# Queries, keys and values of two head pairs per load in an attention and expert kernel

## The chip, the cores and the metric

The kernel runs on one core of a Trainium2 chip. The time is the device time of one execution in microseconds (us); for the kernel before, the median of three runs is 401.37 us, from 398.73 to 402.49 us. The profile was taken from one more execution, which took 402.86 us. TensorE does the matmuls, VectorE (DVE), ScalarE (ACT) and GpSimd (POOL) the elementwise work, and SP issues most DMAs; GpSimd and ScalarE issue a few. All DMAs of the core share 16 DMA engines.

## The reference

Attention with a relative position bias over 8 batches, 8 heads, 576 positions and 64 values per head in float32; its output goes, token by token, through one of 8 experts that a hash of the token's number picks. Cut to what matters:

```python
scores = q @ k.T / sqrt(64) + bias[:, h]       # bias depends on |i - j| alone
attn = softmax(scores)
x = (attn @ v) as rows of 512 per token        # 4608 tokens
e = token_ids * 2654435761 % 8
out[token] = maximum(x[token] @ w1[e], 0) @ w2[e]
```

## The kernel before, in words

Attention works on pairs of heads: 4 pairs in each of 8 batches, 32 pairs (`pairs`, numbered n = 4b + m). Of a head's 576 positions, 512 form the main part, and the last 64 the rest, which are loaded and treated for all heads of a batch together. The main part of one head lies in memory as 2 blocks (NT = 2) of 128 rows of 512 bytes, each row two positions. A tile `qf`, `kf` or `vf` holds one pair, 256 KB in float32, 2 KB in each of 128 partitions, and each has four buffers. `load(n)` fills it with one DMA per head, 128 KB each, so six DMAs per pair, all but two from SP's queue. `load_rest(b)` loads the rest rows: two DMAs of 64 KB each for `qr` and `kr`, four of 32 KB for `vr`, each tile with a single buffer.

The casts to 16 bits follow. `cast_qk(n)` makes `qh` and `kh` (two buffers each), `cast_v(n)` makes `va` (three), both on GpSimd but for the first pair; `cast_rest` is on DVE and `cast_vrest` on GpSimd. TensorE then transposes `qh` and `kh` (`transpose_qk`), DVE copies the transposes out of PSUM (`kt`, `qt`), and TensorE multiplies them into the scores (`products`). ScalarE takes the exponential of five score tiles per pair (g = 0 to 4, `scores`, line 507), DVE multiplies some of it by bias factors (`band`), and TensorE multiplies the result by the values (`av_steps`, line 575). DVE divides by the sums and writes `x_all`.

The order on every engine is written out by hand (`manual_schedule`); each engine works its own list in order, and waits for what the others owe it. The list is made by a loop over the score tiles. At the first score tile of pair n, `pair_start(n)` issues, in this order: the rest rows of the next batch when m = 0, the loads for pair n + 4, the token numbers' loads at n = 4 (`route_load`, six small DMAs), one of ten fills of a table in device memory (`fill_table`, 514 KB, pairs 2 to 11), the casts of queries and keys for pair n + 3, from n = 12 on two scatters of finished rows by GpSimd (`dispatch`), and near the end the loads of the first two experts' weights by GpSimd's queue: w1 of expert 0 at pair 20, w2 at 22, w1 of expert 1 at 25 and w2 at 28. `behind(n, 2)` casts the values of pair n + 1, and `behind` at pairs with m = 1, g = 3 casts the rest rows of the next batch. `early(n, 3)` transposes the queries and keys of pair n + 2. A load into a buffer that is still to be read waits for the cast that reads it, and what stands behind that load in SP's list waits with it.

Before the loop stands a start by hand: the loads of pairs 0 to 3, the bias table's way through device memory (`btr`, and `btb` in three DMAs), constants and first casts. After the loop, the experts' part loads the scattered rows (`x_load`), and for each expert runs two rows of matmuls (lines 859 and 877), with weights two experts ahead.

Of the kernel before, what the change touches and what calls it, by code (L numbers as in the profile page):

```python
# [11 lines left out]
F32 = mybir.dt.float32  # L12
# [19 lines left out]
def kernel(  # L32
# [11 lines left out]
    nc = tc.nc  # L44

    B, H, S, D = q.shape
# [103 lines left out]
    with tc.tile_pool(name="at", bufs=1) as at, tc.tile_pool(  # L150
# [33 lines left out]
        def load(n, which="qkv", eng=None):  # L184
            b, m = pairs[n]
            for key, dst, src in (("q", qf, q), ("k", kf, k), ("v", vf, v)):
                if key not in which:
                    continue
                dst[n] = at.tile([P, 2, NT, 2 * D], F32, name=key + "f",
                                 bufs=4)  # L190
                for hh in range(2):
                    (eng or nc.sync).dma_start(  # L192
                        out=dst[n][:, hh, :, :],
                        in_=bass.AP(
                            src.tensor, (b * H + 2 * m + hh) * S * D,
                            [[2 * D, P], [2 * P * D, NT], [1, 2 * D]],
                        ),
                    )

        def load_rest(b, which="qkv", eng=None):  # L200
            for key, dst, src in (("q", qr, q), ("k", kr, k)):
# [3 lines left out]
                for hh in range(2):  # L205
                    (eng or nc.sync).dma_start(  # L206
                        out=dst[b][:, hh, :],
                        in_=bass.AP(
                            src.tensor, ((b * H + hh) * S + NB4) * D,
                            [[2 * S * D, NPAIR], [2 * D, RU], [1, 2 * D]],  # L210
                        ),
                    )
# [13 lines left out]
        def cast_qk(n, qeng=None, keng=None):  # L226
            for dst, src, name, eng in ((qh, qf, "qh", qeng),
# [4 lines left out]
                    in_=src[n][:, :, :, :].rearrange(  # L232
# [4 lines left out]
        def cast_v(n):  # L237
            nc.gpsimd.tensor_copy(
                out=va[n % 3][:, :, :D],
                in_=vf[n][:, :, :, :].rearrange(  # L240
# [148 lines left out]
        def transpose_rest(b):  # L389
# [10 lines left out]
            for hh in range(2):  # L400
# [6 lines left out]
                        "p c (m u) -> p c m u", m=NPAIR  # L407
# [7 lines left out]
                    "p c (m u) -> p c m u", m=NPAIR  # L415
# [206 lines left out]
        load(0, "k")  # L622
# [12 lines left out]
        load(0, "q")  # L635
# [26 lines left out]
        load(0, "v", nc.scalar)  # L662
        load_band(0, 2, nc.scalar)
        load(1, "qk")
# [31 lines left out]
        load(1, "v")  # L696
        cast_vrest(0)
        load(2)
        load_band(4, H, nc.sync)
        cast_qk(2)  # L700
        load(3)
        nc.sync.dma_start(out=msk[:, :], in_=MSK_d.ap())
        nc.sync.dma_start(out=cnt[:, :], in_=CNT_d.ap())
        nc.sync.dma_start(out=tok[:, :], in_=TOK_d.ap())

# [25 lines left out]
        def pair_start(n):  # L731
# [3 lines left out]
            if n + 4 < NP:  # L735
                load(n + 4)
# [14 lines left out]
            if n == 20:  # L751
                load_w1(0)
            if n == 22:
                load_w2(0)
            if n == 25:
                load_w1(1)
            if n == 28:
                load_w2(1)
# [270 lines left out]
```

## Time and profile before

| What | Value |
|---|---|
| median of 3 runs | 401.37 us |
| the profiled execution, its own time | 402.86 us |
| its span | 401.1 us |
| TensorE busy in the span | 325.7 us (81%) |
| ScalarE, GpSimd, DVE busy | 205.6, 165.0, 158.5 us |
| exponentials (line 507), 160 of them | 152.6 us busy |
| matmuls of the experts (lines 859 and 877) | 72.4 and 72.7 us busy |
| moved by all DMAs | 72.86 MB in 94548 packets |

Attention takes the span's first 229 us or so, the experts the part from 242 us to 391 us. Busy times are added up over the span, so an engine can be full in one stage and waiting in another; the rows below are read by stretches for that reason.

### The profile page before, as it was taken

How to read it: one execution, taken by the hardware profiler on the slowest of the kernel's cores; microseconds unless marked ns; L12 is line 12 of the kernel's file. 1: busy time of each engine (PE TensorE's matmuls, PEld its weight loads, DVE VectorE, ACT ScalarE, POOL GpSimd, SP SyncE). 2: the span in 40 equal slices, each digit the busy share in tenths (PEclk: the TensorE clock that was granted, in tenths of full speed). 3: DMA queues.
4: the chain of work that ended last, by engine and by line, in shares of the span. 5: the costliest groups of instructions: out<-in, count | busy, mean ns of one | idle time of the engine just before them, and what ended most of it. 6: DMA issues, size and time to landing. Idle time of an engine off the chain costs nothing.

```text
span 401.1 us, 9071 instructions
## 1 busy us (share of the span) xinstructions
PE 325.7 (81%) x3680; PEld 205.3 (51%) x3680; DVE 158.5 (40%) x386; ACT 205.6 (51%) x243; POOL 165.0 (41%) x229
## 2 busy tenths in 40 slices
PE   2664997879798697875978609999999999999990
PEld 0232664456565464643645406565757565656650
DVE  1114464876565656544534401314051322223120
ACT  1472995688968788854957403241505041322310
POOL 6132532424468575592566220233242515141231
PEclk9987998899989999988988957999999999999997
DMA  5896958979794858997959042589999999995221
GB/s 152 203 235 170 283 130 200 256 203 265 210 256 135 253 158 180 270 158 203 211 160 168 16 157 88 94 193 158 270 176 226 229 176 266 162 262 112 91 72 61
DMA packets 94548, 72.86 MB, mean 182 GB/s; under 512 B 15223, under 2 KB 85655, under 8 KB 94496
## 3 DMA queue, kind: packets, MB, share of 16 engines
q1 hardware_dynamic: 74720, 40.13, 37.5%
q0 software_dynamic: 17664, 30.96, 36.6%
q10 hardware_dynamic: 2112, 1.09, 1.0%
q8 instruction: 31, 0.51, 0.5%
q14 instruction: 21, 0.17, 0.1%
HBM read 69.47 MB, written 21.03 MB: 226 GB/s over the span
## 4 chain that ended last, share of the span: by engine, by line
PE 56%; DMA 19%; SPq 12%; DVE 5%; issue 3%; POOL 2%; ACT 1%; ACTq 0%; POOLq 0%; DVEq 0%
PE hps L859 17%; PE ops L877 17%; PE px L575 6%; SPq L192 6%; DMA qf<-in_q_dram 5%; PE ps L465 5%; PE ps L442 4%; DMA kf<-in_k_dram 3%; DMA t_xperm<-zx 3%; PE xps L838 2%; DMA vf<-in_v_dram 2%; SPq L218 2%; PE pqk L377 2%; SPq L206 1%; DMA btb<-t_f 1%
## 5 line engine op out<-in xcount | busy, mean ns | idle before, releaser
L507 ACT ACTIVATE att<-ps 128x1024 f16<-128x1024 f32 x160 | 152.6, 1037 | 57.1 <-PE ps L465 44.0
L865 ACT ACTIVATE h<-hps 128x640 f16<-128x640 f32 x64 | 45.0, 704 | 113.4 <-PE hps L859 113.0
L877 PE MATMUL ops<-w2t,h 128*128 128x512 f16 x320 | 72.7, 379 | 0.0
L859 PE MATMUL hps<-xpt,w1t 128*128 128x320 f16 x512 | 72.4, 302 | 0.1
L575 PEld LDWEIGHTS <-att 128*128 128x128 f16 x1408 | 57.5, 101 | 11.6 <-issue 6.8
L885 POOL DMA_INDIRECT out_dram<-ok,xpn x40 | 39.2, 979 | 57.4 <-DVE ok L884 51.3
L575 PE MATMUL px<-va,att 128*128 128x65 f16 x1280 | 61.0, 199 | 1.0 <-issue 0.4
L859 PEld LDWEIGHTS <-w1t 128*128 128x128 f16 x512 | 50.6, 99 | 21.4 <-issue 0.3
L442 PE MATMUL ps<-btb,idents 128*128 128x384 f16 (+1 forms) x256 | 50.0, 283 | 2.2 <-DMA btb<-t_f 1.5
L465 PE MATMUL ps<-qt,kt 64*128 64x512 f16 x256 | 47.1, 414 | 4.5 <-DVE rnk L320 2.0
L600 POOL DMA_INDIRECT t_xperm<-x_all,ds x40 | 40.4, 1010 | 21.0 <-DVE rcp L584 9.4
L230 POOL CAST qh<-qf 128x512 f16<-128x512 f32 x31 | 20.2, 653 | 67.8 <-DMA qf<-in_q_dram 52.2
L877 PEld LDWEIGHTS <-h 128*128 128x128 f16 x320 | 30.7, 98 | 33.5
L884 DVE COPY ok<-ops 128x512 f32<-128x512 f32 x40 | 27.7, 692 | 47.0 <-PE ops L877 47.0
L842 DVE COPY xpt<-xps 128x640 f16<-128x640 f16 x32 | 15.0, 489 | 74.6 <-PE xps L838 60.0
L517 DVE TENSOR_TENSOR att<-att,ebd 128x768 f16<-128x768 f16 x64 | 38.3, 599 | 6.5 <-ACT ebd L540 6.5
L383 DVE COPY kt<-pqk 128x512 f16<-128x512 f16 x32 | 13.6, 425 | 55.9 <-PE pqk L377 46.0
L585 DVE TENSOR_TENSOR x_all<-px,rcp 128x384 f16<-128x384 f32 x64 | 31.4, 491 | 2.2
L442 PEld LDWEIGHTS <-idents 128*128 128x128 f16 x336 | 21.5, 102 | 19.1 <-issue 16.0
L465 PEld LDWEIGHTS <-kt 64*128 64x128 f16 x512 | 16.2, 96 | 29.4 <-issue 22.9
L133 POOL DMA_DIRECT2D w1t<-in_moe_w_dram x8 | 6.5, 807 | 52.3 <-PE xps L838 52.3
L230 POOL CAST kh<-kf 128x512 f16<-128x512 f32 x31 | 19.5, 629 | 13.6 <-DMA kf<-in_k_dram 13.3
(77 smaller groups left out, 264.4 us busy)
## 6 DMA issues: line engine op xcount, KB each, us to landing
kf<-in_k_dram SPq DMA_DIRECT2D x64, 128.0 KB
qf<-in_q_dram SPq DMA_DIRECT2D x64, 128.0 KB
w1t<-in_moe_w_dram POOLq DMA_DIRECT2D x8, 1024.0 KB
w2t<-in_moe_w_dram POOLq DMA_DIRECT2D x8, 1024.0 KB
vf<-in_v_dram SPq DMA_DIRECT2D x62, 128.0 KB
t_xperm<-zx SPq DMA_DIRECT2D x10, 514.0 KB
xpn<-t_xperm SPq DMA_DIRECT2D x8, 642.5 KB
vr<-in_v_dram SPq DMA_DIRECT2D x32, 32.0 KB
```

What stands on the lines that cost most here:

```text
L230: (eng or nc.gpsimd).tensor_copy(out=dst[n][:, :, :, :].transpose([0, 2, 1, 3]), in_=src[n][:, :, :, :].rearrange("p h t (c d) -> p h (t c ...
L442: nc.tensor.matmul(out=out, lhsT=idents[:, which, :], rhs=rhs, start=start, stop=True, skip_group_check=True,)
L465: nc.tensor.matmul(out=ps[:, hh, o : o + rhs.shape[1]], lhsT=lhsT, rhs=rhs, start=not biased and (g < KT or t == 0), stop=True, skip_group ...
L507: nc.scalar.activation(out=att[:, g, :, :], in_=ps[:, :, :], func=AF.Exp, bias=0.0, scale=scale,)
L517: nc.vector.tensor_tensor(out=a, in0=a, in1=ebd[:, 2 * m : 2 * m + 2, 1 - c : 3 - c, :], op=ALU.mult,)
L575: nc.tensor.matmul(out=po, lhsT=lhsT, rhs=rhs, start=(i == 0), stop=(i == len(todo) - 1), skip_group_check=True,)
L585: nc.vector.tensor_tensor(out=x_all[:, b, its[0] : its[0] + ni, :DM].rearrange("p t (m h d) -> p t m h d", h=2, m=NPAIR)[:, :, m, :, :], i ...
L600: sc_in = nc.gpsimd.indirect_dma_start(out=xperm_d.ap()[:, :], out_offset=bass.IndirectOffsetOnAxis(ap=ds2[:, B * t + b : B * t + b + 1], ...
L859: nc.tensor.matmul(out=hps[:, nr, :NR], lhsT=w1h[:, kt, ts(ft, P)], rhs=xt[e][:, kt, ts(nr, NR)], start=(kt == 0), stop=(kt == NPT - 1),)
L865: nc.scalar.activation(out=h1[:, ft, :].rearrange("p (r n) -> p r n", r=NRC), in_=hps[:, :, :NR], func=AF.Relu, bias=0.0, scale=1.0,)
L877: nc.tensor.matmul(out=ops[:, :], lhsT=h1[:, ft, ts(kc, P)], rhs=w2h[:, ft, :], start=(ft == 0), stop=(ft == NFT - 1),)
L885: so = nc.gpsimd.indirect_dma_start(out=out[:, :], out_offset=bass.IndirectOffsetOnAxis(ap=xn[e][:, kc, DM:XW].bitcast(I32), axis=0), in_= ...
```

## The change

A tile `qf`, `kf` or `vf` now holds two pairs (four heads), 4 KB in each partition, with three buffers. A load fills it with one DMA for each of the two blocks T, with four heads in it, 256 KB each; the first two pairs are still loaded as two halves of two heads. In the loop, the loads stand at every second pair: those of queries and keys for pairs n + 6 and n + 7, those of values for n + 4 and n + 5. The casts read their half of the tile. In `load_rest`, the source's order becomes row first, pair of heads second, and the copies behind the rest rows' transposes follow it. The experts' first weights are loaded at pairs 22, 24, 26 and 28 (w1 and w2 of expert 0, w1 and w2 of expert 1). The arithmetic is the same.

```diff
-        def load(n, which="qkv", eng=None):
-            b, m = pairs[n]
+        def load(j, which="qkv", eng=None, h0=0, h1=4):
...
-                dst[n] = at.tile([P, 2, NT, 2 * D], F32, name=key + "f",
-                                 bufs=4)
-                for hh in range(2):
+                if j not in dst:
+                    dst[j] = at.tile([P, 4, NT, 2 * D], F32, name=key + "f",
+                                     bufs=3)
+                for T in range(NT):
                     (eng or nc.sync).dma_start(
-                        out=dst[n][:, hh, :, :],
+                        out=dst[j][:, h0:h1, T, :],
                         in_=bass.AP(
-                            src.tensor, (b * H + 2 * m + hh) * S * D,
-                            [[2 * D, P], [2 * P * D, NT], [1, 2 * D]],
+                            src.tensor, (4 * j + h0) * S * D + 2 * P * D * T,
+                            [[2 * D, P], [S * D, h1 - h0], [1, 2 * D]],
                         ),
                     )
@@ load_rest
-                            [[2 * S * D, NPAIR], [2 * D, RU], [1, 2 * D]],
+                            [[2 * D, RU], [2 * S * D, NPAIR], [1, 2 * D]],
@@ cast_qk (and cast_v with vf)
-                    in_=src[n][:, :, :, :].rearrange(
+                    in_=src[n // 2][:, 2 * (n % 2) : 2 * (n % 2) + 2].rearrange(
@@ transpose_rest, twice
-                        "p c (m u) -> p c m u", m=NPAIR
+                        "p c (u m) -> p c m u", m=NPAIR
@@ the start
-        load(0, "k")
+        load(0, "k", None, 0, 2)
...
-        load(0, "q")
+        load(0, "q", None, 0, 2)
...
-        load(0, "v", nc.scalar)
+        load(0, "v", nc.scalar, 0, 2)
         load_band(0, 2, nc.scalar)
-        load(1, "qk")
+        load(0, "qk", None, 2)
...
         load_rest(0, "v")
-        load(1, "v")
+        load(0, "v", None, 2)
         cast_vrest(0)
-        load(2)
+        load(1, "qk")
         load_band(4, H, nc.sync)
         cast_qk(2)
-        load(3)
+        load(1, "v")
         nc.sync.dma_start(out=msk[:, :], in_=MSK_d.ap())
         nc.sync.dma_start(out=cnt[:, :], in_=CNT_d.ap())
         nc.sync.dma_start(out=tok[:, :], in_=TOK_d.ap())
+        load(2, "qk")
@@ pair_start
             if b + 1 < B and m == 0:
                 load_rest(b + 1)
-            if n + 4 < NP:
-                load(n + 4)
+            if n % 2 == 0 and n + 6 < NP:
+                load(n // 2 + 3, "qk")
+            if n % 2 == 0 and n + 4 < NP:
+                load(n // 2 + 2, "v")
...
-            if n == 20:
-                load_w1(0)
-            if n == 22:
-                load_w2(0)
-            if n == 25:
-                load_w1(1)
-            if n == 28:
-                load_w2(1)
+            if n >= 22 and n % 2 == 0 and n < 30:
+                (load_w2 if n % 4 == 0 else load_w1)((n - 22) // 4)
```

## Rows read from the trace of the kernel before

**Rows 1.** Stretches: length, busy us of engines (x instructions), TensorE's clock, DMA share, GB/s.

```profile
core 0: us, PE busy (x) PEld busy (x) DVE busy (x) ACT busy (x) POOL busy (x), PEclk, DMA share, GB/s
0.00:40.00 40.00, 20.50 (x166) 9.86 (x167) 10.11 (x29) 16.91 (x21) 12.63 (x33) 0.88 0.74 190
40.00:230.00 190.00, 154.81 (x2523) 103.75 (x2521) 105.72 (x285) 143.68 (x159) 99.75 (x141) 0.93 0.79 196
40.00:110.00 70.00, 59.78 (x982) 39.98 (x980) 42.70 (x118) 58.41 (x67) 26.89 (x45) 0.94 0.86 221
110.00:150.00 40.00, 33.84 (x558) 22.81 (x559) 23.93 (x63) 30.98 (x36) 28.94 (x40) 0.96 0.70 201
...
70.00:80.00 10.00, 7.95 (x104) 4.73 (x103) 8.37 (x24) 6.82 (x9) 4.30 (x8) 0.83 1.07 257
90.00:100.00 10.00, 9.72 (x177) 6.73 (x173) 6.87 (x18) 8.76 (x11) 4.85 (x8) 1.00 1.14 266
120.00:130.00 10.00, 8.91 (x157) 6.01 (x153) 5.84 (x14) 8.29 (x11) 8.72 (x12) 1.00 0.46 137
...
245.00:391.00 146.00, 145.90 (x966) 88.51 (x965) 40.08 (x67) 45.05 (x64) 47.81 (x51) 1.00 0.79 171
```

**Rows 2.** Waits, whole span: engine, line, what was waited for, us, times, longest.

```profile
POOL qh L230 <- DMA qf<-in_q_dram: 52.2, 17, 7.6
...
POOL kh L230 <- DMA kf<-in_k_dram: 13.3, 17, 3.9
```

**Rows 3.** TensorE in order of time: start, length, instructions, idle before.

```profile
23.00 0.40 PE L377 MATMUL pqk<-idents,kh 128*128 128x128 f16 x4 [2.10 <-POOL kh L230]
```

**Rows 4.** GpSimd in order of time, same columns.

```profile
111.46 0.61 POOL L230 CAST kh<-kf 128x512 f16<-128x512 f32 x1 [0.65 <-DMA kf<-in_k_dram]
...
153.58 0.84 POOL L133 DMA_DIRECT2D w1t<-in_moe_w_dram  x1
```

**Rows 5.** Instructions on the query tile: count, shortest, median, longest in ns.

```profile
L192 SPq DMA_DIRECT2D qf<-in_q_dram x64: 367/468/2227, 1.7 to 200.9; - x64
```

**Rows 6.** Waits of SP's queue: the first whole span, the second 13 to 30 us.

```profile
SPq L192 <- POOL va L238: 10.3, 4, 3.7
...
SPq L703 <- DMA btb<-t_f: 0.9, 1, 0.9
```

**Rows 7.** SP's queue in order of time: start, length, issues.

```profile
21.34 0.47 SPq L654 DMA_DIRECT2D btb<-t_f  x1
...
27.32 0.34 SPq L703 DMA_DIRECT2D cnt<-t_cnt  x1
```

**Rows 8.** The chain that ended last, in order of time: start, us, what.

```profile
30.27 4.72 DMA kr<-in_k_dram
...
62.25 4.76 DMA t_xperm<-zx
67.03 5.34 DMA qf<-in_q_dram
...
154.26 9.02 DMA vf<-in_v_dram
...
193.74 9.70 DMA kf<-in_k_dram
```

**Rows 9.** SP's DMA queue on the page: packets, MB, share of 16 engines' span.

```profile
q1 hardware_dynamic: 74720, 40.13, 37.5%
```

**Rows 10.** Groups by shape, copies behind the rest rows' transposes: busy us, mean ns.

```profile
L401 DVE COPY kzr<-pr 64x256 f16<-64x256 f16 x16 | 4.6, 289 | 1.5 <-PE pr L393 1.3
...
L410 DVE COPY qtr<-pr 128x256 f16<-128x256 f16 x8 | 2.3, 292 | 0.1
```

**Rows 11.** DVE in order of time, the rest rows' cast.

```profile
35.11 0.29 DVE L250 CAST krh<-kr 128x256 f16<-128x256 f32 x1 [2.25 <-DMA kr<-in_k_dram]
```

**Rows 12.** The chain on the page, shares of the span by engine.

```profile
PE 56%; DMA 19%; SPq 12%; DVE 5%; issue 3%; POOL 2%; ACT 1%; ACTq 0%; POOLq 0%; DVEq 0%
```

More of the change, by code (lines that the diff above doesn't have):

```diff
@@ L239, in cast_v @@
                 out=va[n % 3][:, :, :D],
-                in_=vf[n][:, :, :, :].rearrange(
+                in_=vf[n // 2][:, 2 * (n % 2) : 2 * (n % 2) + 2].rearrange(
                     "p h t (c d) -> p (h t c) d", c=2
@@ L414, in transpose_rest @@
                 in_=pr[:, 1, :, :].rearrange(
-                    "p c (m u) -> p c m u", m=NPAIR
+                    "p c (u m) -> p c m u", m=NPAIR
                 ),
```

## The prediction

> **What bounds the kernel now.** I read the stretches of the span first, then the chain of waits, then the queues. In the stretches [rows 1] the reader is to see two halves. From 245 us on, the experts keep TensorE busy for 145.90 of 146 us; no row says that loads of queries, keys or values reach there, and I leave it as it is. From 40 to 230 us, attention, TensorE is busy for only 154.81 of 190 us (0.81), while the DMA engines stand at 0.79. Neither is full on average. But both are nearly full at times: TensorE 0.97 in 90 to 100 us, and the DMA engines 1.07 and 1.14 in 70 to 80 and 90 to 100. A stage in which two resources take turns at being full is short of work in flight, not of rate.
>
> The waits say who is short: GpSimd stands 52.2 us in 17 waits before its cast of the queries, and 13.3 us before that of the keys, each time for a DMA [rows 2]. The casts feed TensorE's transposes. At 23.00 us TensorE had been idle for 2.10 us until the cast keys of pair 2 came [rows 3]. Even where the DMA engines have room (110 to 150 us, share 0.70), the cast at 111.46 us waited for keys again [rows 1, 4].
>
> Why are the loads late? Two reasons, both on SP's queue. First, an issue takes a median of 468 ns on SP [rows 5], and a pair needs six of them, 2.8 us, besides 8 smaller ones per batch and a table fill. Second, an issue waits for the landing of the eighth one before it: the load of `cnt` at 27.32 us waited 0.9 us for the `btb` of 21.34 us, and from that one to it there are six L192 issues, `msk` and `cnt` itself, eight steps [rows 6, 7]. The chain repeats this: the fill issued at 62.25 us lands 4.76 us later and lets the query load of 67.03 us go, which takes 5.34 us to land, and so on [rows 8]. So eight issues of mostly 128 KB, some 1 MB, share one landing of about 5 us, and any small DMA in the eight costs a whole place. Where the weights come in, at 153.58 us [rows 4], landings grow to 9.02 and 9.70 us [rows 8], and then the lead of the query loads, about two pairs, isn't enough.
>
> **The change, part by part.**
>
> *Larger loads.* Three issues per pair instead of six: 3 x 0.468 = 1.4 us of SP time per pair less. For the issue of 256 KB no row exists; the nearest are 128 KB (468 ns) and the 768 KB `btb` of 21.34 us, 0.47 us [rows 5, 7]. They agree, so I take 0.47. The transfer itself: the rows stay 512 bytes long, so the same number of packets. A price change per packet has no row; the queue's 74720 packets take 37.5% of 16 engines' 401.1 us, 32 ns each [rows 9]. I take no change, and bound it at 10% either way: q, k and v are 55296 packets, 111 us of all 16 engines, so 11 us of DMA time, most of it under other work. What grows is the bytes that eight outstanding issues hold, up to 2 MB.
>
> *Deeper buffers for queries and keys.* Three buffers of two pairs each instead of four of one; a load for pairs n+6 and n+7 now stands at pair n, where the one for n+4 stood. SP runs ahead to whichever buffer is not free: now SP spends 10.3 us waiting for the value casts [rows 6], since value buffer n is freed only in pair n-1. After the change the values for n+4, n+5 need the cast of n-1, which lies in pair n-2, and the queries and keys have five pairs of lead when SP is not behind. At some 5.3 us a pair that is over 25 us, against landings of up to 9.70 us. So GpSimd's waits go nearly entirely. Late next is TensorE's own order, with ScalarE's exponentials beside it (143.68 us of the 190 [rows 1]).
>
> *Rest rows.* The order in the source becomes rows first, heads second. The DVE copies behind the transposes read with a stride then; 16 + 8 copies of 0.29 us [rows 10]: between nothing and twice that, 7 us in all on an engine that is 0.56 busy, taken at 0. For the load: the 64 KB of `kr` took 4.72 us to land, against 5.34 us for 128 KB of queries [rows 8], and DVE stood 2.25 us for it in order, with TensorE behind [rows 11]. I take 1.5 us saved at the start, from 0 to 3.
>
> [...]
>
> *Start.* Pair 2's keys now come with pair 3's, 512 KB more ahead of the cast. At the start's 190 GB/s [rows 1] that is up to 2.8 us, taken 2, on the path at 23.00 us; pair 3 then finds its data there, and I count 1 back. The rest rows of batch 1 have 1 MB more ahead of them on SP's queue: up to 5.5 us at the same rate, though two L192 issues fewer; I take 3, less the 1.5 above. Sum of the start: +2.5, from -1 to +7.
>
> *Weights.* Expert 0's loads move two pairs later, w1 of expert 1 one. GpSimd pays the same issue, 0.84 us for that of 153.58 [rows 4]. By pair 22, SP should have issued nearly all query loads, so the landings of 9 us meet full buffers. They're needed by 245 us, with 50 us to spare, and I cost them at 0.
>
> *The stage.* With the feed in place, what does TensorE reach? [...] (154.8 - 3) / 0.90 = 168.7 us instead of 190: -21.3. The DMA engines must then carry 0.79 x 190 = 150 us in 169, a share of 0.89, below the 1.07 and 1.14 seen.
>
> Sum: -21.3 + 2.5 = -18.8. The profiled execution took 402.86 us for a span of 401.1, so 384.1; it stands 1.5 above the median of 401.37, so **383** beside that median.
>
> **Rivals.**
>
> *The DMA engines remain the bound where they're busy.* From 40 to 110 us their share is 0.86 [rows 1] with the table fills in it, and fuller queues then only lengthen each landing. Against it: 1.07 and 1.14 in two stretches. Then only 110 to 230 us gains: TensorE's 95.0 us there at 0.90 take 105.6 instead of 120, -14.4, and with +2.5 about 389.5 beside the median; 388 to 396 with a smaller gain in it.
>
> *Fully fed.* If 0.95 is held, 160 us, -30 and +2.5: 374; 369 to 378.
>
> *Nothing moves.* The issues that go away were hidden, and the waits only change their name. Against it: SP's queue holds 12% of the chain and the DMAs 19% [rows 12]. Then 397 to 405. [...]
>
> *Slower: dearer packets.* Each issue walks four heads 147 KB apart instead of two blocks 64 KB apart of one head. If a packet of these loads took 40% more than 32 ns, 111 us would become 155, and the stage's 150 us of DMA work 190 or so, all the time there is; with the start's +2.5 and some misses beyond, 408. It decides only above some 35%; below that it eats into the gain. For it: nothing in the rows. Against it: the packets keep length and count.
>
> **Chances.** Within 1% (397.4 to 405.4) is about what a measurement can't tell from no change. My forecast, 378 to 388: 0.42. DMA-bound, 388 to 397: 0.23. Fully fed: 0.13. Nothing moves: 0.13. Slower: 0.09. So faster 0.78. The range of 8 in 10 reaches from 371, most of the fully fed case, to 400, a part of no change. Within the gaining cases the start's bounds (-1 to +7) and 10% on packets move the time by no more than that.
>
> **What would show it.** Right: L192 has 100 issues on SP instead of 190, still near 0.47 us each; GpSimd's waits before L230 fall from 65.5 us to under 15; TensorE's share in attention is near 0.90, DMA's near 0.89; attention ends near 211 us instead of 230; the experts' 146 us unchanged. Wrong: GpSimd waits as long as now at longer landings (DMA-bound); the start's transposes or DVE's rest casts wait over 7 us more; packets above 32 ns; or TensorE's share stays near 0.81 with GpSimd's waits gone, the stage then being bound by its own order.

## The result, and the profile after

The changed kernel took a median of 396.0 us in 17 runs (392.68 to 399.67), the kernel before 402.04 us in 17 beside it: a ratio of 0.9862, 95% interval [0.9829, 0.9895]. That is 1.4% or some 5.5 us, where 383 was forecast and 371 to 400 given as the range. The same file, run again later on two chips, gave 0.9546 [0.9503, 0.9588] and 0.9622 [0.9579, 0.9665], 18.1 and 15.5 us, where 18.8 was forecast. So two questions are open: what kept the gain small in the first comparison, and whether the forecast was right where its number came out. Ratios are those of undisturbed runs alone; one experiment (e3_depth) had one such run and has no ratio.

The profiled execution of the changed kernel took 398.55 us for a span of 396.8. Its stretches, in the columns of [rows 1]:

```profile
40.00:230.00 190.00, 154.51 (x2516) 102.12 (x2513) 115.33 (x285) 142.78 (x158) 100.64 (x139) 0.92 0.76 192
40.00:110.00 70.00, 58.61 (x958) 39.26 (x956) 44.94 (x113) 55.21 (x63) 27.05 (x44) 0.93 0.91 242
...
240.00:386.00 146.00, 145.90 (x966) 88.47 (x964) 40.08 (x67) 45.05 (x64) 47.99 (x51) 1.00 0.79 171
```

Against [rows 1], the reader is to see that TensorE's share from 40 to 230 us did not move (154.51 of 190 after, 154.81 before). The experts' full stretch starts 5 us earlier and is the same 145.90 us. GpSimd's waits, over the whole span, columns as in [rows 2]:

```profile
POOL qh L230 <- PE pqk L377: 39.8, 23, 5.0
...
POOL kh L230 <- DMA kf<-in_k_dram: 4.0, 3, 1.8
POOL qh L230 <- DMA qf<-in_q_dram: 3.9, 2, 2.5
```

The 65.5 us for DMAs [rows 2] have become 7.9. GpSimd now waits for TensorE, 39.8 us of it until a cast tile is given back: the feed is ahead of its user. On the page, SP's DMA queue (packets, MB, share of 16 engines' span) and the chain of waits, to be read against [rows 9] and [rows 12]:

```profile
q1 hardware_dynamic: 73616, 40.13, 37.6%
...
PE 67%; DMA 11%; DVE 7%; SPq 5%; issue 4%; ACT 2%; POOL 1%; POOLq 0%; DVEq 0%; ACTq 0%
```

A packet takes 0.376 x 16 x 396.8 us / 73616 = 32 ns, as before. TensorE's part of the chain rose from 56 to 67%, SP's queue and the DMAs fell from 31 to 16%. What is still late in the changed kernel stands in its order of time, DVE and TensorE (start, length, instruction, idle before):

```profile
9.72 0.39 PE L393 MATMUL pr<-idents,krh 128*128 128x128 f16 x2 [2.42 <-DVE krh L250]
...
35.99 0.40 PE L393 MATMUL pr<-idents,krh 128*128 128x128 f16 x2 [4.36 <-DVE x_all L585]
...
64.89 0.18 DVE L287 TENSOR_SCALAR te<-te 128x40 int32<-128x40 int32 x1 [2.67 <-DMA te<-in_moe_token_ids_dram]
...
66.01 0.38 PE L377 MATMUL pqk<-idents,kh 128*128 128x128 f16 x4 [3.24 <-DVE x_all L585]
```

The rest rows of batch 1 are transposed at 35.99 us after 4.36 us of idle TensorE, and at 64.89 us DVE stands 2.67 us for the small token-number loads, with TensorE idle 3.24 us behind it. Both are small loads that now stand behind larger ones in SP's queue. They were late before as well, though. The rest rows, in the trace of the kernel before:

```profile
36.63 0.39 PE L393 MATMUL pr<-idents,krh 128*128 128x128 f16 x2 [5.06 <-DVE x_all L585]
```

DVE waited 1.53 us for the token numbers there, and 2.40 us in a later trace of the same kernel (f6_before).

### The profile page after: what moved, and what is told of

The parts are those of the page before. It is cut to its first block, busy times and chain, and to the rows that moved or that the text cites. A ratio compares the mean times of both kernels' runs of the same rounds, so it can differ in the third digit from the quotient of the medians.

```text
span 396.8 us, 8968 instructions
## 1 busy us (share of the span) xinstructions
PE 326.2 (82%) x3680; PEld 204.6 (52%) x3680; DVE 169.7 (43%) x386; ACT 205.3 (52%) x243; POOL 165.5 (42%) x229
## 3 DMA queue, kind: packets, MB, share of 16 engines
q1 hardware_dynamic: 73616, 40.13, 37.6%
## 4 chain that ended last, share of the span: by engine, by line
PE 67%; DMA 11%; DVE 7%; SPq 5%; issue 4%; ACT 2%; POOL 1%; POOLq 0%; DVEq 0%; ACTq 0%
PE hps L856 18%; PE ops L874 17%; PE px L575 10%; PE ps L465 8%; PE ps L442 6%; PE pqk L377 4%; PE xps L835 3%; SPq L192 3%; ACT att L507 2%; DMA t_xperm<-zx 2%; DMA qr<-in_q_dram 2%; DVE x_all L585 2%; DMA vf<-in_v_dram 2%; PE ps L499 2%; DMA btb<-t_f 1%
## 5 line engine op out<-in xcount | busy, mean ns | idle before, releaser
L575 PEld LDWEIGHTS <-att 128*128 128x128 f16 x1408 | 56.8, 101 | 11.0 <-issue 5.9
L575 PE MATMUL px<-va,att 128*128 128x65 f16 x1280 | 60.7, 198 | 1.2 <-DVE qt L386 0.5
L856 PEld LDWEIGHTS <-w1t 128*128 128x128 f16 x512 | 50.5, 99 | 21.4 <-issue 0.3
L442 PE MATMUL ps<-btb,idents 128*128 128x384 f16 (+1 forms) x256 | 49.5, 280 | 3.9 <-DMA btb<-t_f 2.9
L600 POOL DMA_INDIRECT t_xperm<-x_all,ds x40 | 41.7, 1042 | 21.1 <-DVE rcp L584 11.1
L465 PE MATMUL ps<-qt,kt 64*128 64x512 f16 x256 | 47.6, 423 | 3.3 <-ACT att L507 3.3
L517 DVE TENSOR_TENSOR att<-att,ebd 128x768 f16<-128x768 f16 x64 | 42.5, 664 | 7.9 <-ACT ebd L540 7.9
L230 POOL CAST qh<-qf 128x512 f16<-128x512 f32 x31 | 19.0, 614 | 46.4 <-PE pqk L377 39.8
L238 POOL CAST va<-vf 128x512 f16<-128x512 f32 x32 | 19.7, 617 | 33.8 <-PE px L575 23.0
L383 DVE COPY kt<-pqk 128x512 f16<-128x512 f16 x32 | 13.6, 425 | 43.8 <-PE pqk L377 41.6
L442 PEld LDWEIGHTS <-idents 128*128 128x128 f16 x336 | 21.0, 101 | 21.7 <-issue 17.2
L465 PEld LDWEIGHTS <-kt 64*128 64x128 f16 x512 | 16.0, 96 | 27.5 <-issue 20.8
L133 POOL DMA_DIRECT2D w1t<-in_moe_w_dram x8 | 6.5, 812 | 51.8 <-PE xps L835 51.8
```

Of the source, the lines that this page charges most:

```text
L442: nc.tensor.matmul(out=out, lhsT=idents[:, which, :], rhs=rhs, start=start, stop=True, skip_group_check=True,)
L465: nc.tensor.matmul(out=ps[:, hh, o : o + rhs.shape[1]], lhsT=lhsT, rhs=rhs, start=not biased and (g < KT or t == 0), stop=True, skip_group ...
L517: nc.vector.tensor_tensor(out=a, in0=a, in1=ebd[:, 2 * m : 2 * m + 2, 1 - c : 3 - c, :], op=ALU.mult,)
L575: nc.tensor.matmul(out=po, lhsT=lhsT, rhs=rhs, start=(i == 0), stop=(i == len(todo) - 1), skip_group_check=True,)
L600: sc_in = nc.gpsimd.indirect_dma_start(out=xperm_d.ap()[:, :], out_offset=bass.IndirectOffsetOnAxis(ap=ds2[:, B * t + b : B * t + b + 1], ...
L856: nc.tensor.matmul(out=hps[:, nr, :NR], lhsT=w1h[:, kt, ts(ft, P)], rhs=xt[e][:, kt, ts(nr, NR)], start=(kt == 0), stop=(kt == NPT - 1),)
```

## The experiments

Theory at the start: the third buffer lets SP run ahead, and the small loads behind it come late (the rest rows, the token numbers), while the cast tiles, still two of each, hold GpSimd. Rival: the DMA engines are the bound. A third theory came from the traces themselves: TensorE's results reach the other engines late. Each series ran on one chip, with the kernel before beside it.

### First series: loads, weights, depth and size alone

**e1_noload** takes the load work away after the first six pairs; the casts then read those pairs' tiles again, so its output is of other data.

```diff
-            if n % 2 == 0 and n + 6 < NP:
-                load(n // 2 + 3, "qk")
-            if n % 2 == 0 and n + 4 < NP:
-                load(n // 2 + 2, "v")
+            if n == 0:
+                load(2, "v")
...
-                    in_=src[n // 2][...
+                    in_=src[n // 2 % 3][...
```

> The changed kernel without the loads of queries, keys and values for pairs 6 to 31; the casts read the first six pairs' tiles again. 23 MB of loads are gone, all else is issued as before. Theory A (attention is bound by the engines' own order, about 6 us a pair, once the loads are ahead): the time falls by 2 to 8 us from the changed kernel's 396, to 388 to 394, mostly from 40 to 100 us, and TensorE's share from 100 to 200 us stays near 0.85. Theory B (the loads are still the bound, by the DMA engines' rate): attention runs at TensorE's 0.95, 20 us or more less, to 376 or under.

Measured: 387.5 us, 0.9621 [0.9544, 0.9698]. With hardly any queries, keys and values left to load, this chip gives 3.8%. One stretch of its trace:

```profile
100.00:170.00 70.00, 60.15 (x1030) 40.10 (x1022) 47.44 (x113) 58.13 (x65) 51.47 (x68) 0.98 0.30 75
```

The DMA engines are at 0.30 there, and TensorE still reaches only 60.15 of 70 us, 0.86. So a lack of transfer rate is not what holds it.

**e2_weights** is the kernel before with only the weights' loads moved.

```diff
-            if n == 20:
-                load_w1(0)
...
-            if n == 28:
-                load_w2(1)
+            if n >= 22 and n % 2 == 0 and n < 30:
+                (load_w2 if n % 4 == 0 else load_w1)((n - 22) // 4)
```

> The kernel before with only the first two experts' weights moved to pairs 22, 24, 26 and 28. Theory A1 (the gain lies from 170 to 220 us because the weights no longer meet the last loads): 2 to 5 us faster than before, ratio 0.988 to 0.995. Rival A2 (the deeper buffers took up the collision, the weights' place is worth nothing): within 1 us of before, ratio 0.997 to 1.003.

Measured: 397.98 us, 0.992 [0.9875, 0.9965]. The move, costed at 0, is worth 0.8% by itself.

**e3_depth** is the kernel before, with its loads of 128 KB, six buffers, and the changed kernel's lead: depth alone.

```diff
-                                 bufs=4)
+                                 bufs=6)
...
-            if n + 4 < NP:
-                load(n + 4)
+            for i in (6, 7) if n % 2 == 0 else ():
+                if n + i < NP:
+                    load(n + i, "qk")
+            for i in (4, 5) if n % 2 == 0 else ():
+                if n + i < NP:
+                    load(n + i, "v")
...
+        load(4, "qk")
+        load(5, "qk")
```

> The kernel before, still with one pair per tile and 128 KB per DMA, but with six buffers and the loads issued where the changed kernel issues them (queries and keys for pairs n+6, n+7 and values for n+4, n+5, at even n). Depth alone. If the places in SP's queue bind (eight issues share a landing), depth can't be filled and the gain is under 2 us, ratio 0.995 to 1.0. If depth is what gave the 6 us, ratio 0.985 to 0.99 with 128 KB DMAs too.

Measured: no ratio, so what depth alone does stays open.

**e4_size** is the changed kernel with two buffers instead of three for queries and keys, so with 256 KB loads and the lead of before. The weights' new places and the rest rows' new order are in it too.

```diff
-                                     bufs=3)
+                                     bufs=3 if key == "v" else 2)
...
-        load(2, "qk")
...
-            if n % 2 == 0 and n + 6 < NP:
-                load(n // 2 + 3, "qk")
+            if n % 2 == 0 and n + 4 < NP:
+                load(n // 2 + 2, "qk")
```

> The changed kernel with two buffers of two pairs for queries and keys (four pairs, as many as the kernel before had) and their loads issued for n+4, n+5 beside the values'. Size alone, without depth. If size gave the gain: 396 or so, ratio 0.983 to 0.99. If depth gave it: GpSimd waits for queries again, over 15 us, and the ratio is 0.993 to 1.005.

Measured: 388.28 us, 0.9683 [0.961, 0.9756], faster than either case had expected. Its GpSimd waits, and TensorE at its first two rest transposes and behind them:

```profile
POOL qh L230 <- DMA qf<-in_q_dram: 31.8, 7, 9.7
POOL kh L230 <- DMA kf<-in_k_dram: 15.2, 11, 2.4
```

```profile
9.65 0.39 PE L393 MATMUL pr<-idents,krh 128*128 128x128 f16 x2 [2.00 <-DVE krh L250]
...
32.44 0.29 PE L393 MATMUL pr<-idents,krh 128*128 128x128 f16 x2 [1.26 <-DVE x_all L585]
...
38.27 0.61 PE L377 MATMUL pqk<-idents,kh 128*128 128x128 f16 x4 [3.53 <-POOL kh L230]
```

GpSimd still waits 47.0 us for loads, against 65.5 [rows 2] and 7.9, and yet the kernel is within 0.6% of the one without loads (which keeps the 1 MB for pairs 4 and 5 at the start). So most of those waits can't have been on the path. The second rest transposes come at 32.44 us instead of 35.99, since the 1 MB no longer stands ahead of the rest rows. But TensorE then idles 3.53 us for the next keys, and the third rest transposes come at 60.41 us, where the changed kernel has 60.48: the 3.5 us are gone again.

### Second series: the late small loads, the cast tiles, the start

```diff
-            if n == 4:
+            if n == 2:
                 route_load()
```

**e5_te** is that edit, the token-number loads two pairs earlier. 

> The changed kernel with the token numbers' loads at pair 2 instead of pair 4. In the changed kernel's trace they land at 64.8 us, DVE waits 2.67 us for them in order, and TensorE stands 3.24 us before the transposes at 66.01 us. Theory A (the deeper prefetch put small urgent loads behind it in SP's queue, and DVE's wait is on the path): 2.5 to 5 us faster than the changed kernel, 391 to 394, ratio to before 0.972 to 0.980. Rival B (the wait is taken up by slack within the next pairs): within 1.5 us of the changed kernel, ratio 0.982 to 0.99.

Measured: 392.89 us, 0.9747 [0.969, 0.9803]; DVE's wait of 2.67 us is gone.

```diff
-                dst[n] = at.tile([P, KT, 2, D], F16, name=name, bufs=2)
+                dst[n] = at.tile([P, KT, 2, D], F16, name=name, bufs=4)
```

**e6_castbufs** is that edit, four cast tiles for two. 

> The changed kernel with four buffers instead of two for the cast queries and keys, so that GpSimd's casts no longer start exactly when TensorE's transposes end, which is when DVE copies these transposes and goes on to line 517 and, at a batch's edge, to the rest rows' casts. Theory A (the casts now run beside DVE's work and slow it: line 517 664 ns against 599, the rest casts 636 against 371): line 517 falls below 630 ns, TensorE's idle time before the rest transposes from 1.91 us each to 1.5 or less, the time by 2 to 5 us, ratio 0.972 to 0.982. Rival B (the collision is off the path): DVE's times fall, the total stays within 1.5 us, ratio 0.982 to 0.99. Rival C: the casts only collide elsewhere, no change in either.

Measured: 393.15 us, 0.9759 [0.9706, 0.9811].

```diff
-        load(2, "qk")
...
                 load_rest(b + 1)
+            if n == 0:
+                load(2, "qk")
```

**e8_start** is that edit, the rest rows of batch 1 ahead of the 1 MB. 

> The changed kernel with the start's loads of queries and keys for pairs 4 and 5 issued behind batch 1's rest rows instead of ahead of them. Theory A (the 1 MB ahead of the rest rows costs the start 3 to 4 us): the first rest transposes come at about 32.5 us instead of 36.0 and the time falls by 2 to 4 us, ratio 0.975 to 0.982. Rival B (the token numbers' landing near 65 us takes it up again): the transposes come earlier, but DVE waits longer for the token numbers and the time falls by less than 1.5 us, ratio 0.982 to 0.99.

Measured: 397.36 us, 0.9881 [0.9832, 0.9931]. The rest transposes came at 32.89 us, as in e4_size, but TensorE then idled 2.73 us for the next keys, at 37.91 us, and DVE waited 2.3 us for the token numbers. It is the slowest of its series: on this chip e5_te is worth more than the earlier rest rows.

**e9_size_rest** is e4_size with the order of the rest rows of before.

```diff
-                            [[2 * D, RU], [2 * S * D, NPAIR], [1, 2 * D]],
+                            [[2 * S * D, NPAIR], [2 * D, RU], [1, 2 * D]],
...
-                    "p c (u m) -> p c m u", m=NPAIR
+                    "p c (m u) -> p c m u", m=NPAIR
```

> The kernel with large loads and two buffers for queries and keys (388.3 us, ratio 0.968) with the rest rows' old order: four heads outermost in the source, and the contiguous copies behind their transposes. [...]

Measured: 391.67 us, 0.9706 [0.9646, 0.9766]. Its first rest transposes:

```profile
13.10 0.40 PE L393 MATMUL pr<-idents,krh 128*128 128x128 f16 x2 [5.33 <-DVE krh L250]
```

They come 3.5 us after those of e4_size (9.65), so the new order does bring the first rest rows sooner. At the fourth rest transposes 0.5 us of it is left (84.59 and 84.09 us). Over the whole kernel 0.9706 and 0.9683, on two chips, can't be told apart.

Read against 0.9862, e5_te and e6_castbufs look like 1% each. But 0.9862 was measured on another occasion, and the next series showed that this is not a fair comparison.

### Third series: repairs together

**e10_te_cast** is e5_te and e6_castbufs together; **e11_size_te_cast** adds the two buffers of e4_size; **e12_oldweights** is the changed kernel with the weights' loads back at pairs 20, 22, 25 and 28; **e13_start_te** is e8_start and e5_te together. Their edits are those above (the weights' in reverse).

> The changed kernel with both repairs: the token numbers' loads at pair 2, and four buffers for the cast queries and keys. Alone they gave ratios of 0.975 and 0.976 against the changed kernel's 0.986, so about 4.5 and 4 us. Theory A (two separate costs, both on the path): they add up, 0.961 to 0.969, 386 to 390 us. Rival B (each only uncovers the other, or the same slack): 0.970 to 0.977.

> The kernel with large loads and two buffers for queries and keys (0.968) with both repairs. In it the token numbers already came in time, and the casts collided less. Theory A: at most 2 us better, 0.962 to 0.970, since only the collision of line 517 (675 ns) is left to take away. Rival B (deeper buffers are needed once the collisions are gone): no better than 0.970.

> The changed kernel with the experts' first weights back at pairs 20, 22, 25 and 28. The weights' new places alone gave the kernel before 0.992. Theory A (with five pairs of lead the loads no longer mind the weights' traffic): within 1.5 us of the changed kernel, 0.982 to 0.990. Rival B (the weights' new places are what gave more than half of the gain in this kernel too): 0.990 to 0.998.

> The changed kernel with batch 1's rest rows ahead of the loads for pairs 4 and 5 at the start (alone 0.988, no gain), and the token numbers' loads at pair 2 (alone 0.975). Theory A (the start's gain of 3 us was taken up by the wait for the token numbers): now it shows, 0.965 to 0.971. Rival B (the start's gain is lost in the wait for the next keys, 2.73 us at 37.91 us in that kernel's trace): no better than the token numbers alone, 0.972 to 0.979.

Measured: e10_te_cast 379.74 us, 0.9571 [0.953, 0.9612]; e11_size_te_cast 377.25 us, 0.9499 [0.945, 0.9548]; e12_oldweights 382.38 us, 0.9647 [0.9598, 0.9696]; e13_start_te 380.5 us, 0.9595 [0.9552, 0.9638]. All four lie below what was expected of them from the ratio of 0.986. What fits least is e12_oldweights: it has none of the repairs and a part of the change less, and was 3.5% faster than before, where the changed kernel had given 1.4%. Either the old place of the weights is better here, against e2_weights, or this chip is another case. So the changed kernel itself had to run again.

### Fourth series: the changed kernel again, and each repair beside it

**f1_after** is the changed kernel without an edit; **f3_size** is e4_size, **f4_te** is e5_te, **f5_castbufs** is e6_castbufs, each again.

> The changed kernel itself, beside its variants on one chip. The series so far ran on three chips, each against the kernel before on the same chip, and the changed kernel itself was in none of them. If the ratio is the same on every chip: 0.983 to 0.990. If it depends on the chip (one series gave its variants 0.957 to 0.965): anywhere from 0.96 to 0.99, and only differences within a series count.

> The kernel with large loads and two buffers for queries and keys, on the same chip as the changed kernel. If the deeper prefetch costs what it seemed to (0.968 against 0.986): 4 to 9 us faster than the changed kernel here. If that was the chip: within 2 us.

> The changed kernel with the token numbers' loads at pair 2, on the same chip as the changed kernel. Theory A: 2.5 to 5 us faster than the changed kernel here. Rival: the 4.5 us found against the changed kernel's ratio were a difference of chips; within 1.5 us here.

> The changed kernel with four buffers for the cast queries and keys, on the same chip as the changed kernel. Theory A (the casts beside DVE's work cost time on the path): 2 to 5 us faster than the changed kernel here. Rival: within 1.5 us, DVE's times fall off the path.

Measured: f1_after 381.38 us, 0.9546 [0.9503, 0.9588]; f3_size 376.93 us, 0.9444 [0.94, 0.9489]; f4_te 382.06 us, 0.9554 [0.9507, 0.96]; f5_castbufs 380.95 us, 0.9534 [0.9492, 0.9576]. Three things follow. The changed kernel gains about what was forecast on this chip. The token numbers' place and the cast tiles are worth nothing that these runs can show. The third buffer is a loss: two buffers are 1.2% faster (376.93 against 381.38), and the intervals don't meet; e11_size_te_cast against e10_te_cast points the same way. The second rest transposes in f1_after, and then in f3_size with what TensorE waits for next:

```profile
36.96 0.28 PE L393 MATMUL pr<-idents,krh 128*128 128x128 f16 x2 [3.43 <-DVE x_all L585]
```

```profile
33.47 0.28 PE L393 MATMUL pr<-idents,krh 128*128 128x128 f16 x2 [1.26 <-DVE x_all L585]
...
38.23 0.40 PE L377 MATMUL pqk<-idents,kh 128*128 128x128 f16 x4 [2.47 <-POOL kh L230]
```

The lead of f3_size is 3.5 us here, but 1.9 us at the third rest transposes (59.74 against 61.65 us), since the wait for keys takes a part of it back, and 4.8 us at the fourth (84.17 against 88.97). From 60 to 90 us f1_after has a granted clock of 0.88 and waits 1.9 us for the token numbers; f3_size has 0.94 and no such wait. So the 1 MB ahead of the rest rows doesn't explain the loss by itself, and e8_start, which takes away just that, was the slowest of its series. Where the third buffer costs its 4.5 us stays open.

### Fifth series: both kernels' traces on one chip

**f6_before** and **f7_after** are the two kernels without an edit.

> The kernel before, unchanged, for its trace on the same chip as the changed kernel's. Ratio to itself 1.00, within 0.5%. Theory of the late completion (VectorE sees the last product of a pair late on some chips): before waits no more than 6.4 us in 30 to 225 us for TensorE ahead of its reciprocal, as in the trace that the prediction rests on, whatever the chip, since its pairs have idle places between them. Rival (the waits belong to the schedule, not to the chip): 6.4 us again within 1 us.

> The changed kernel, unchanged. Theory of the late completion: where the ratio is near 0.986, the trace shows 10 us or more of waits of VectorE's reciprocal for TensorE in 30 to 225 us (10.8 + 3.5 us in the trace on record), and a batch of four pairs takes about 24 us between two rest transposes; where the ratio is near 0.955, it shows none, and a batch takes about 21.5 us. Rival (the difference is one of the kernel before, which is slower on some chips): the ratio differs while the changed kernel's waits and batches are the same. A ratio between 0.965 and 0.977 speaks against two kinds of chip.

Measured: f6_before 397.82 us, 1.0004 [0.9968, 1.004]; f7_after 382.11 us, 0.9622 [0.9579, 0.9665]. In the two traces the last exponentials of the attention end at 218.1 and 204.7 us: 13.4 of the 13.6 us by which the spans differ (393.2 and 379.6) lie in the attention. VectorE's waits ahead of its reciprocal from 30 to 225 us, first in the changed kernel's trace of the first comparison, then in f6_before and f7_after:

```profile
DVE rcp L584 <- PE px L575: 14.2, 22, 3.4
DVE rcp L584 <- PE ps L465: 10.8, 9, 2.4
DVE rcp L584 <- PE ps L442: 3.5, 3, 1.4
```

```profile
DVE rcp L584 <- PE px L575: 13.8, 25, 1.2
```

```profile
DVE rcp L584 <- PE px L575: 11.7, 23, 1.6
```

The reciprocal needs only the products of L575. A wait that ends with a later matmul (L465, L442) means that DVE was let go after TensorE had, by its rows, gone on to other work. There were 14.3 us of those in the first comparison, and none here in either kernel. ScalarE shows it too: its exponentials need scores, which no matmul of L575 writes, and yet some of its waits in that first trace, from 30 to 210 us, end with one. There are none such in f7_after:

```profile
ACT att L507 <- PE px L575: 4.8, 7, 1.8
```

A batch of four pairs, taken between the third and the eighth rest transposes, lasts 24.8 us in the first trace of the changed kernel and 22.2 in f7_after, and 25.4 and 24.9 us in the two traces of before. So the rival of f7_after, that the changed kernel's waits and batches are the same everywhere, falls. The rival of f6_before, 6.4 us of such waits again, falls too: the kernel before has 3.5 + 2.9 us of them in its first trace and none in f6_before. Late results go with the occasion, not with the schedule.

## Why the prediction was right and wrong

**Larger loads: right.** 100 issues on L192 instead of 190, packets at 32 ns. The issue itself has a median of 0.51 us for queries and keys, a little over the 0.47 taken, and of 0.69 for values, half as much again:

```profile
L192 SPq DMA_DIRECT2D qf<-in_q_dram x34: 367/506/1672, 1.7 to 165.6; - x34
L192 SPq DMA_DIRECT2D vf<-in_v_dram x32: 367/688/3887, 15.9 to 176.6; - x32
```

**GpSimd's waits gone: right as a fact,** 65.5 us to 7.9, under the 15 forecast. As a reason it was too much. With 47.0 us of them left, e4_size kept the gain, and f3_size, with 34.5, beat the changed kernel. What counts are the waits that TensorE stood behind, and in the kernel before those were few. From 30 to 225 us, its waits for GpSimd's cast keys and, for comparison, for DVE ahead of the rest transposes:

```profile
PE pr L393 <- DVE x_all L585: 19.2, 7, 5.1
...
PE pqk L377 <- POOL kh L230: 7.4, 4, 2.8
```

Of the 7.4 us, 6.1 stand at 167 us and later, where the weights come in. In the changed kernel TensorE waits for cast keys once, at 23.92 us. The waits ahead of the rest transposes stay: 15.8 us of them in its first trace, 16.6 in f7_after.

**The start: the sum had the wrong sign.** 2.5 us of loss were forecast; the second rest transposes stand at 35.99 us, 0.6 us before those of the first trace of before (36.63), and in f7_after 0.6 us before f6_before's (36.77 and 37.41). The keys of pair 2 were right: TensorE idles 4.05 us for them instead of 2.10, where 2 was taken, and the wait for pair 3 is gone, 1.33 us in the first trace of before, where 1 was counted back. The 3 us for the 1 MB ahead of the rest rows were not: TensorE waits 4.36 us there, and had waited 5.06 before. Without the 1 MB the rest rows come 3.5 us sooner (e4_size, f3_size), and the next keys take all or half of it back.

The new order of the rest rows brings the first rest transposes to 9.72 us, from 11.86 in the trace of before, 2.1 us, and e4_size against e9_size_rest shows 3.5. Both are above the 1.5 taken, and the second is above the 3 at the end of its range; why these rows land sooner, no row shows. Little of it is kept: behind these transposes TensorE waits for the bias table, 2.86 us instead of 1.47, and goes on at 15.12 us instead of 15.87. The copies behind the transposes pay for the stride, but on DVE, where there is room (115.33 of 190 us busy). In the changed kernel, groups by shape, as [rows 10]:

```profile
L401 DVE COPY kzr<-pr 64x256 f16<-64x256 f16 x16 | 6.8, 422 | 1.3 <-PE pr L393 1.0
...
L410 DVE COPY qtr<-pr 128x256 f16<-128x256 f16 x8 | 3.4, 425 | 0.1
```

That is 422 and 425 ns for 289 and 292, 24 x 0.13 = 3.2 us, inside the bound of 7.

**The weights at 0: too low** by some 3 us. e2_weights alone gave 0.8%, and e12_oldweights stands 0.7% above e10_te_cast on the same chip (382.38 against 379.74), which differs from it also in two edits that gave nothing in the fourth series. The landings of 9.02 and 9.70 us [rows 8] were on the path before. The prediction saw that the deeper buffers would cover them and didn't count what moving them is worth.

**The stage at 0.90: this is the step that failed.** The forecast let TensorE go from 0.81 to 0.90 once the feed was in place, 21.3 us less from 40 to 230 us. That gave the feed some 18 us of TensorE's idle time, and its waits for cast keys, 7.4 us, are less than half of that. No row behind that sum shows its 0.90 for the stage, or its 3 us less of busy time; what the runs show is 0.81 and, over the whole attention, 0.5 us more in the first comparison, and 0.89 and 5.3 us less in f7_after against f6_before. In the first comparison the feed came and the share stayed: 154.51 of 190 us, 0.81, and the attention ended 4.8 us earlier (225.3 and 220.5 us). Where the number came out, luck had a part. From 40 us to the end of the attention f6_before takes 178.1 us and f7_after 164.7, with TensorE at 0.85 and then 0.89: the stage gave 13.4 us there, the weights' share included, not 21.3. That the medians still differ by 15.5 us is also owed to the start, which cost nothing where 2.5 was forecast: two misses of opposite sign.

Where the gain lies, the rest transposes of the seventh and eighth batch show, in the trace of before and then in the changed kernel's first:

```profile
158.53 0.28 PE L393 MATMUL pr<-idents,krh 128*128 128x128 f16 x2 [1.26 <-DVE x_all L585]
...
187.85 0.40 PE L393 MATMUL pr<-idents,krh 128*128 128x128 f16 x2 [4.74 <-DVE x_all L585]
```

```profile
162.06 0.28 PE L393 MATMUL pr<-idents,krh 128*128 128x128 f16 x2 [1.91 <-DVE x_all L585]
...
184.65 0.28 PE L393 MATMUL pr<-idents,krh 128*128 128x128 f16 x2 [1.92 <-DVE x_all L585]
```

Between the two, where the first weights are loaded, the kernel before takes 29.3 us (32.4 in f6_before), the changed kernel 22.6 (23.2 in f7_after). Up to there the changed kernel is 3.5 us behind in the first comparison and 3.6 us ahead in the fifth series. So this one batch of eight holds more than the first comparison's 4.8 us, and 9.3 of the 13.4 us of the fifth series. The prediction named the place, and then spread the gain evenly over the stage. The batch is as short with either remedy alone: 21.4 us in e2_weights, 22.0 in e12_oldweights. e2_weights reaches it at 162.27 us, 3.7 us later than the first trace of before, on another chip, so 0.8% is what is left of that over the whole kernel.

How far a fed stretch gets depends on the occasion. One stretch, 100 to 170 us, first in the changed kernel's first trace, then in f7_after:

```profile
100.00:170.00 70.00, 58.29 (x951) 37.76 (x949) 44.97 (x107) 54.86 (x61) 49.26 (x65) 0.95 0.74 199
```

```profile
100.00:170.00 70.00, 64.01 (x1139) 43.99 (x1137) 49.38 (x122) 63.89 (x72) 54.32 (x71) 1.00 0.84 226
```

TensorE is at 0.83 and 0.91 (0.90 in f1_after); ScalarE does 61 and 72 activations of the same kernel in the same 70 us (70 in f1_after). In the first trace the 0.90 isn't reached even though the loads are there, and in e1_noload it isn't reached without loads (0.86). What the traces show in its place are late results. The same place of the program, TensorE, DVE and ScalarE in order of time, first there:

```profile
149.98 0.22 PE L575 MATMUL px<-vt,rr 128*128 128x130 f16 x1
...
150.99 0.50 PE L442 MATMUL ps<-btb,idents 128*128 128x384 f16 x2
151.76 0.18 DVE L584 RECIPROCAL rcp<-px 128x4 f32<-128x4 f32 x1 [1.36 <-PE ps L442]
151.84 1.94 ACT L507 ACTIVATE att<-ps 128x1024 f16<-128x1024 f32 x2 [0.68 <-PE ps L442]
...
152.55 0.38 PE L377 MATMUL pqk<-idents,kh 128*128 128x128 f16 x4 [1.06 <-DVE x_all L585]
```

and in f1_after:

```profile
122.51 0.22 PE L575 MATMUL px<-vt,rr 128*128 128x130 f16 x1
...
122.98 0.17 DVE L584 RECIPROCAL rcp<-px 128x4 f32<-128x4 f32 x1
...
123.86 0.39 PE L377 MATMUL pqk<-idents,kh 128*128 128x128 f16 x4
```

The sequence and the lengths are the same. The last product ends, by its row, at 150.20 and 122.73 us. The reciprocal starts 1.56 us later in the one and 0.25 us later in the other, and the transposes, which need its tile back, 2.35 us and 1.13 us later. In the first trace TensorE idles 1.06 us for it; ScalarE, waiting for scores, idles 0.68 us at the same time.

Every kernel profiled in the first two series has such waits on DVE, 5.3 to 16.2 us of them, and the first trace of before has 6.4; in the traces of the last three series there are none, but for 0.3 us in one. So much is shown. That they are the cause of the small gain is argued, and the traces don't bear out that they are all of it. The attention from its start to the end of the last exponential, in the columns of [rows 1], for before and after in the first comparison, then for f6_before and f7_after:

```profile
0.00:225.25 225.25, 173.47 (x2643) 112.06 (x2643) 113.49 (x307) 160.59 (x179) 110.53 (x172) 0.92 0.79 199
0.00:220.49 220.49, 174.01 (x2643) 111.43 (x2643) 124.68 (x307) 160.21 (x179) 111.06 (x172) 0.91 0.80 203
```

```profile
0.00:218.12 218.12, 172.08 (x2649) 112.14 (x2649) 118.27 (x309) 159.57 (x179) 113.44 (x172) 0.93 0.80 205
0.00:204.68 204.68, 166.74 (x2649) 109.72 (x2649) 124.47 (x309) 158.76 (x179) 111.44 (x172) 0.94 0.86 218
```

TensorE does nearly the same matmuls in all four. In the first comparison its busy time rose by 0.5 us and its idle time fell by 5.3 (51.8 to 46.5); in the fifth series the one fell by 5.3 us and the other by 8.1 (46.0 to 37.9). So of the 8.7 us by which the two gains differ, 5.9 are busy time, the changed kernel's granted clock being 0.91 in the one and 0.94 in the other, and only 2.8 are idle time, the part in which waits for late results show. Nor do the waits order the times within a series: e5_te has the most of them, 16.2 us, and 0.9747, e8_start 15.5 us and 0.9881. The granted clock alone doesn't tell the occasions apart either: e4_size and f3_size are one kernel, at 0.98 and 0.97 up to the end of the attention, which comes at 210.8 us in the one and 199.2 in the other.

Not settled, then, is why. The granted clock reads 1.00 around both of the places above (145 to 155 us in the one, 116 to 126 in the other), the highest it has in the traces, where it also stands at 0.50 (in that of before from 34.45 to 37.80 us); ends of matmuls are modelled, so the rows can't say whether the results were late or the matmuls themselves longer than drawn. Chip and hour changed together, so which of them matters isn't separated.

**The rivals.** *DMA-bound* put the gain after 110 us, and that is where most of it is. f6_before, f7_after and e1_noload in turn:

```profile
40.00:110.00 70.00, 61.74 (x986) 41.20 (x982) 42.69 (x116) 57.68 (x65) 26.87 (x44) 0.91 0.82 223
110.00:170.00 60.00, 48.57 (x835) 33.45 (x836) 38.09 (x95) 46.94 (x53) 42.54 (x57) 0.94 0.81 213
```

```profile
40.00:110.00 70.00, 61.03 (x1012) 41.05 (x1010) 48.55 (x124) 59.05 (x67) 28.04 (x45) 0.96 0.92 241
110.00:170.00 60.00, 55.27 (x978) 37.77 (x974) 42.41 (x104) 54.82 (x62) 46.97 (x63) 1.00 0.85 224
```

```profile
40.00:110.00 70.00, 60.16 (x1004) 40.16 (x1001) 49.76 (x124) 57.76 (x66) 31.73 (x50) 0.97 0.34 92
```

From 40 to 110 us ScalarE does 65 activations before and 67 after, from 110 to 170 us 53 and 62. But its reason falls: with the DMA engines at 0.34, e1_noload does 66 from 40 to 110 us, and e4_size on the same chip 68 with the DMA engines at 0.91. So the forecast spread the gain over a part of the stage that the loads didn't hold back. *Dearer packets* falls at 32 ns. *Nothing moves* falls at each ratio. *Fully fed* (0.95 held) wasn't reached in any of these stretches. What did come, in the first comparison, is the case that the prediction named at its end and gave no chance of its own: TensorE near 0.81 with GpSimd's waits gone. Its time, 396.0, lies at the edge of the range given to DMA-bound (388 to 397), whose reason is not what held it.

## What to carry to other kernels

Look first for the one batch that takes longer than its neighbours: here it held most of what could be gained. A wait of a feeding engine is worth what the engine behind it idles for; price the feed from the fed engine's idle time, 7.4 us here, not from the feeder's 65.5 us. More bytes per issue and a deeper queue are two changes: without the deeper queue the kernel was 1.2% faster, and depth alone was not measured. A load that is moved ahead of another makes the other late: what the rest rows gained without the 1 MB, 3.5 us, the next keys lost, wholly or in part. And the same pair of kernels gave 0.986, 0.962 and 0.955 on three occasions, each within a third to half a percent either way: variants that differ by a percent are compared side by side, as f4_te and f5_castbufs against f1_after, or not at all.

## What was not expected of the hardware

- Results of TensorE that DVE sees late, in some series only, as above: at the twelve waits of the changed kernel's first trace its reciprocal starts 0.3 to 1.9 us after the row of the last product ends.
- DVE's instructions take longer on some occasions, it seems where GpSimd's casts stand beside them. In the first traces of the two kernels the rest casts (L250) with no such cast beside them, 12 of 32, take 278 to 295 ns, the others 293 to 745; the multiplications of L517 without one, 77 of 128, take 543 to 616 ns, the others 540 to 1145, so not every cast does it. The queries' rest cast had a mean of 371 ns before and 636 in the changed kernel, and L517 599 and 664. In f6_before, without the change, they are 524 and 650, so it isn't the change as such. It isn't the DMAs either: in e1_noload L517 takes 672. With four cast tiles, which move the casts, they fall to 533 and 611 in f5_castbufs. That the casts are the cause isn't shown: no run here takes them away.
